# Attention and two feed-forward layers on one Trainium2 core: more weight splits ahead of use, and weight rooms that change hands

## The chip, the cores and the metric

One NeuronCore of a Trainium2 chip runs the whole program. The metric is the device time of one launch in microseconds (us).

## The reference, cut to what matters

```python
def reference(...):
    attn = attention with tanh-capped scores        # 4 batches, 12 heads, 448 tokens, 64 wide
    x = attn as [1792, 768]
    x = (silu(x @ w_gate) * (x @ w_val)) @ w_out     # dense layer, 1536 wide
    do_compute = x @ w_skip > 0                      # tokens that enter the expert layer
    e_idx = argmax(x @ w_route)                      # one of 8 experts for each such token
    for e in range(8):                               # w1[e]: 768 x 1024, w2[e]: 1024 x 768
        h = maximum(x[e_idx == e] @ w1[e], 0)
        y[e_idx == e] = softmax weight * (h @ w2[e])
    out = x, plus y where do_compute
```

## The kernel before

The program runs attention and the dense layer interleaved over four batches, and the expert layer as its last part. Everything is issued in an order written out by hand; each engine runs its own instructions in that order.

The expert layer works in **slots**. A slot holds up to 128 gathered tokens of one expert; a **paired slot** holds 64 tokens of each of two experts. This input uses six slots in this order: 0 to 3 with one expert each, then two paired slots. Slots 0 and 1 are written out word by word in the list `LATE`, mixed with the routing of the last batch (`choose`, `ranks`, `tiles`, `places`, `gates`, `at`, `entries`, `listed`), which runs on VectorE and whose result, the token lists, is needed by the four gathers for the later slots. Slots 2 and up are issued by `slot`, with `so["auto"]` set.

The weights of one expert are eight **pieces** of 768 KB, [128, 1536] in float32: four for w1 (used by `first`, 9 matmuls of 512 columns in float32r) and four for w2 (used by `second`, 12 matmuls of 384 columns). Between them, hidden rows or the next slot's token rows are turned on TensorE (`turn_h`, `turn_x`) and copied out by ScalarE and VectorE. Number the pieces in the order of use: 0 to 7 belong to slot 0, 8 to 15 to slot 1, 16 to 23 and 24 to 31 to slots 2 and 3, 32 to 63 to the two paired slots.

A piece of slots 0 to 3 goes through four steps. `load_next` issues its load on SyncE into a free raw room (`so["raw"]`, 8 of them: three 1536-column pieces of older tiles and five new ones) and puts it on `held`. `split_next` takes the first of `held`, casts it on ScalarE to a high part `gh` (line 1014), subtracts on VectorE to a low part `gl` (line 401), frees the raw room, and puts the two parts on `ready`. The parts take one of seven pairs of rooms (`so["pair"]`); three of the pairs come from the pool "early". `piece`, called by `first` and `second`, takes the first of `ready`; the pair is free again after the matmuls (`used`). A piece of a paired slot **stays whole**: it passes from `held` to `ready` with no cast and no subtraction, is used in float32 straight from its raw room, two pieces (one of each expert) at a time, and frees the raw room only after its matmuls. `first` and `second` then issue half as many columns of weights at a time, two experts side by side.

The lists fill in two ways. In `LATE` the word `split` calls `split_next`. In `slot`, each call of `piece` splits at most one piece, and only while `ready` holds fewer than `AHEAD` = 5.

```python
n = 1
while so["auto"] and held and len(ready) < AHEAD and (not held[0][1] or n and so["pair"]):
    n -= held[0][1]
    split_next()
if not ready:
    split_next()
return ready.pop(0)
```

Seven pieces are split before `LATE` begins, and `LATE` holds nine more splits, so that the last use of slot 1 finds `ready` empty afterwards. A piece is loaded as soon as a raw room is free, but pieces 16 and up wait for the experts of the later slots (`experts`).

Of the kernel before, what the change touches and what calls it, by code (L numbers as in the profile page):

```python
# [7 lines left out]
F32 = mybir.dt.float32  # L8
F32R = mybir.dt.float32r
# [25 lines left out]
AHEAD = 5  # L35
# [30 lines left out]
    chain store  # L66
""".split()
LATE = """
    choose first1 count ranks first2 hidden0 lows0 tiles first3 experts second0 hidden1 lows1 split second1 places
    split second2 rows1 gates split second3 finish0 first0 at split first1 entries split first2 listed0 halves0 split  # L70
    first3 listed1 gather gather gather gather second0 halves1 split second1 rows2 split second2 split second3 finish1
""".split()


# [1 line left out]
def tile_attn_moe_moe(  # L76
# [26 lines left out]
    PIECE = 1536  # L103
# [31 lines left out]
    count = const.tile([T, E], F32, name="count")  # L135
    fit = const.tile([T, 6, E], F32, name="fit")
    early = const.tile([T, FETCHED], F32, name="early")
# [23 lines left out]
    def scratch(room):  # L161
        used = [0]

        def take(*shape):
            n = 1
            for d in shape:
                n *= d
            a = room[:, used[0]:used[0] + n]
            used[0] += n
            assert used[0] <= room.shape[1]  # L170
            if len(shape) == 1:
                return a
            names = " ".join("abc"[:len(shape)])
            return a.rearrange(f"p ({names}) -> p {names}", **dict(zip("abc", shape)))

        return take
# [41 lines left out]
    def gates(b):  # L218
        gt, sh = gate[:, NC * b:NC * b + NC], rt["sh"]
        nc.scalar.activation(out=sh, in_=sh, func=ACTF.Exp)  # L220
        yield V.tensor_reduce(gt, sh, axis=AX.X, op=ALU.add)
        yield V.tensor_scalar(gt, gt, EPS, None, op0=ALU.add)
        yield V.reciprocal(gt, gt)
# [148 lines left out]
    def slot_pieces(e_reg):  # L372
        a = [
            (w1[bass.ds(e_reg, 1), 128 * kk:128 * (kk + 3), 512 * half:512 * half + 512], 3)
            for half in range(F2 // 512) for kk in range(0, KD, 3)
        ]
        return a + [(w2[bass.ds(e_reg, 1), 128 * f:128 * (f + 2)], 2) for f in range(0, KF2, 2)]

    def load_piece(raw, piece):
        src, n = piece  # L380
        nc.sync.dma_start(
            out=raw.rearrange("p (k f) -> p k f", k=n), in_=src.rearrange("o (k p) f -> p (o k) f", p=128)
        )
# [3 lines left out]
    def expert(src):  # L387
        return nc.values_load(src, engines=SP, min_val=0, max_val=E - 1)

    def pieces_of(s):  # L390

        if s < FETCHED:
            return [(p, True) for p in slot_pieces(expert(early_i[0:1, s:s + 1]))]
        if s < MAXWHOLE:
            return [(p, True) for p in slot_pieces(expert(es_i[0:1, s:s + 1]))]
        o = MAXWHOLE + 2 * (s - MAXWHOLE)
        both = zip(*(slot_pieces(expert(es_i[0:1, o + i:o + i + 1])) for i in range(2)))
        return [(p, False) for ps in both for p in ps]

    def split_low(engine, low, full, high):  # L400
        engine.tensor_tensor(low, full, high.bitcast(F32), op=ALU.subtract)  # L401
# [25 lines left out]
    def whole(exact):  # L427
        with ExitStack() as ph:

            def pools(side):  # L430
                stack = ph.enter_context(ExitStack())

                def pool(name, bufs, **kw):
                    kw.setdefault("reuse_waits", "tile")
                    return stack.enter_context(tc.tile_pool(name=name, bufs=bufs, side=side, **kw))

                return stack, pool
# [466 lines left out]
            so = {"raw": [], "pair": [], "xg": [], "auto": False}  # L904

            def open_early():
                qks[0][0].close()
                right.close()
                _, pool = pools("right")
                p = pool("early", 1)  # L910
                psum = pool("ps_e", 1, space=PSUM)
                so["raw"] += [x[:, 0:PIECE] for x in pair_room + [head_room]]
                so["pair"] += [[p.tile([128, PIECE], F32R, name=f"{n}{i}") for n in ("gh", "gl")] for i in range(3)]
                so["odd"] = p.tile([128, PIECE], F32R, name="gl3")
                so["xg"] += [p.tile([128, DM], F32, name=f"xg{i}") for i in range(FETCHED)]
                so["x"] = [p.tile([128, KD, 128], F32R, name=n) for n in ("xgh", "xgl")]
                so["h"] = [[p.tile([128, KF2 // 2, 128], F32R, name=f"{n}{i}") for n in ("rh", "rl")] for i in range(2)]
                so["room"] = p.tile([128, 1024], F32, name="big_room")[0:T]
                so["row"] = p.tile([128, S], F32, name="row2")
                so["ph"] = [psum.tile([128, 512], F32, name=f"ph{i}") for i in range(2)]  # L920
                so["tp"] = [psum.tile([128, 512], F32, name=f"tp{i}") for i in range(2)]
                for xg in so["xg"]:
                    nc.gpsimd.memset(xg, 0.0)
# [62 lines left out]
            def turn_h(half, later=None, n=1):  # L986
                src = so["hid"][:, 512 * half:512 * half + 512]
                if n == 1:
                    turned(*so["h"][half], src, later)
                else:  # L990
                    turned(so["h32"][:, KF2 // 2 * half:KF2 // 2 * (half + 1)], None, src)


            coming, todo, held, ready = [], [], [], []

            def load_next():
                while so["raw"] and not todo:
                    if not coming:
                        return False
                    todo.extend(pieces_of(coming.pop(0)))  # L1000
                if not so["raw"]:
                    return False
                piece_, parted = todo.pop(0)
                held.append((so["raw"].pop(0), parted))
                load_piece(held[-1][0], piece_)
                return True

            def split_next():
                raw, parted = held.pop(0)
                if not parted:  # L1010
                    ready.append((raw,))
                    return
                wh, wl = parts = so["pair"].pop(0)
                nc.scalar.copy(wh, raw)
                split_low(nc.vector, wl, raw, wh)
                so["raw"].append(raw)
                ready.append(parts)
# [9 lines left out]
            def piece():  # L1027
                while load_next():
                    pass

                n = 1
                while so["auto"] and held and len(ready) < AHEAD and (not held[0][1] or n and so["pair"]):
                    n -= held[0][1]
                    split_next()
                if not ready:
                    split_next()
                return ready.pop(0)
# [75 lines left out]
            at = {load_part: 8}  # L1113
# [149 lines left out]
            for word in OPENING:  # L1263
                name = word.rstrip("0123456789")
                x = int(word[len(name):])
# [36 lines left out]
            b, last, take = B - 1, so["last"], scratch(so["late"][0:T])  # L1302

            def all_of(*chains):
                return lambda: [any(False for _ in chain()) for chain in chains]
# [13 lines left out]
            def list_(b0):  # L1319
                for b in range(b0, b0 + 2):  # L1320
                    listed(pl, rhs_[b % 2], rt["rv"][:, NC * b:NC * b + NC], b == 0, b == B - 1)
                    if b < 2:
                        put(b + 2, rhs_[b])
                if b0:
                    to = lists[:, :, FETCHED:]
                    V.tensor_tensor(to, to, pl.rearrange("p (a s) -> p a s", a=2), op=ALU.add)
                    V.tensor_copy(idx[:, FETCHED:], to[:, 0])

            def experts_known():
                yield from experts(take)  # L1330
                coming.extend(order[FETCHED:])
                while load_next():
                    pass

            order = list(range(NWHOLE)) + [MAXWHOLE + i for i in range(NPAIRS)]
            gathered = iter(order[FETCHED:])

# [6 lines left out]
            while load_next():  # L1344
# [4 lines left out]
                "places": all_of(lambda: places(rank, take)), "at": all_of(lambda: last_at(take, room)),  # L1349
                "entries": all_of(entered), "experts": all_of(experts_known),  # L1350
                "listed0": lambda: list_(0), "listed1": lambda: list_(2),
                "gates": all_of(lambda: gates(b)), "split": split_next,
                "hidden0": lambda: turn_h(0, 0), "hidden1": lambda: turn_h(1, 1),
                "lows0": lambda: split_low(V, *lows.pop(0)), "lows1": lambda: split_low(V, *lows.pop(1)),
                "gather": next_gathered, "finish0": lambda: finish(0), "finish1": lambda: finish(1),
# [28 lines left out]
    with tc.manual_schedule():  # L1384
# [57 lines left out]
        with tc.If(big > 0) as cmp:  # L1442
            whole(True)
        with cmp.Else():
            whole(False)
# [31 lines left out]
```

## Time and profile before

| what | value |
|---|---|
| median of 3 runs | 983.2 us (978.3 to 983.58) |
| the profiled execution, its own time | 982.64 us |
| its span, first to last instruction | 980.9 us |
| TensorE busy | 898.1 us (92%) |
| VectorE, ScalarE, GpSimd busy | 580.1, 465.1, 99.1 us |
| mean granted TensorE clock | 0.96 of full speed |
| DMA | 161.55 MB, mean 165 GB/s |

The span lies 1.74 us below the execution's own time. Times in the rows are counted from the start of the span. The granted clock is 1.00 at 2.4 GHz and 0.50 at 1.2 GHz; a stretch with a value between them had some of both. A busy TensorE is not TensorE at its peak, and matmul rows overlap, so steps are read from start to start.

### The profile page before, as it was taken

What the parts mean: (1) busy time and instruction counts of PE and PEld (TensorE: products, weight loads), DVE (VectorE), ACT (ScalarE), POOL (GpSimd) and SP (SyncE); (2) the same over time, 40 slices, a digit from 0 to 9 for tenths busy, and PEclk for the clock granted to TensorE, in tenths of its full rate; (3) what the DMA queues carried; (4) which work ended last, traced back from release to release, by engine and by line L of the source; (5) the groups of instructions that cost most, each with busy time, mean ns of one, the idle gap of its engine ahead of it and who ended that gap; (6) DMA issues with size and microseconds to landing.
All of it is one profiled execution on the core that took longest, in us unless ns stands there. A gap on an engine that the chain in (4) does not pass through costs nothing. (4 is left out here: it accounts for less than half of the span.)

```text
span 980.9 us, 12535 instructions
## 1 busy us (share of the span) xinstructions
PE 898.1 (92%) x4664; PEld 676.4 (69%) x4664; DVE 580.1 (59%) x906; ACT 465.1 (47%) x553; POOL 99.1 (10%) x66
## 2 busy tenths in 40 slices
PE   6899999999999999999999999999999775665984
PEld 2236787776788888778888888999987663544521
DVE  2768899998377666557666743565664943332000
ACT  5887667656464556446555532333342341313100
POOL 1000000000022221212221220000101020000000
PEclk9999999999999999999999999999999988667998
DMA  6996888898764344257343235453376654332894
GB/s 134 195 262 177 221 240 233 227 256 214 185 154 110 84 125 125 57 115 178 94 110 106 65 84 130 134 198 125 90 223 194 211 174 164 108 131 96 310 391 159
DMA packets 226020, 161.55 MB, mean 165 GB/s; under 512 B 158860, under 2 KB 186508, under 8 KB 225936
## 3 DMA queue, kind: packets, MB, share of 16 engines
q1 hardware_dynamic: 224048, 157.12, 57.1%
q0 software_dynamic: 960, 3.16, 0.9%
q8 instruction: 43, 0.70, 0.3%
q14 instruction: 41, 0.34, 0.1%
q10 hardware_dynamic: 928, 0.23, 0.1%
HBM read 140.01 MB, written 22.02 MB: 165 GB/s over the span
## 5 line engine op out<-in xcount | busy, mean ns | idle before, releaser
L748 PE MATMUL mo<-xhl,wh 128*128 128x448 f32 x576 | 215.1, 373 | 0.0
L750 PE MATMUL mo<-xhl,wl 128*128 128x448 f32 x576 | 210.4, 365 | 0.0
L749 PE MATMUL mo<-xhl,wh 128*128 128x448 f32 x576 | 210.3, 365 | 0.0
L401 DVE TENSOR_TENSOR wl<-raw,wh 128x768 fp32r<-128x768 f32 x108 | 117.1, 1084 | 69.8 <-ACT wh L735 69.0
L735 ACT CAST wh<-raw 128x768 fp32r<-128x768 f32 x108 | 89.9, 833 | 76.5 <-PE mo L749 49.5
L748 PEld LDWEIGHTS mo<-xhl,wh 128*128 128x128 f32 x576 | 108.1, 188 | 22.2 <-issue 11.0
L750 PEld LDWEIGHTS mo<-xhl,wl 128*128 128x128 f32 x576 | 108.2, 188 | 8.9 <-DVE wl L401 0.2
L749 PEld LDWEIGHTS mo<-xhl,wh 128*128 128x128 f32 x576 | 108.3, 188 | 7.9
L748 PE MATMUL mo<-hh,wh 128*128 128x448 f32 x288 | 108.2, 376 | 1.1 <-ACT x L795 1.1
L750 PE MATMUL mo<-hh,wl 128*128 128x448 f32 x288 | 105.3, 366 | 0.0
L749 PE MATMUL mo<-hl,wh 128*128 128x448 f32 x288 | 105.3, 366 | 0.0
L787 ACT ACTIVATE s<-mo 128x448 f32<-128x448 f32 x48 | 26.1, 544 | 110.6 <-PE mo L750 107.7
L535 ACT ACTIVATE arena<-ps,inv_sb 112x896 f32<-112x896 f32 x72 | 68.8, 1008 | 4.9 <-PE ps L525 4.9
L542 ACT ACTIVATE arena<-arena,cap_sb 112x1792 f32<-112x1792 f32 x36 | 64.6, 1793 | 1.1
L748 PEld LDWEIGHTS mo<-hh,wh 128*128 128x128 f32 x288 | 54.1, 188 | 11.8 <-issue 4.9
L570 POOL TENSOR_TENSOR sums<-arena 112x896 f32<-112x896 f32 x11 | 23.2, 2111 | 385.7 <-ACT arena L542 385.7
L750 PEld LDWEIGHTS mo<-hh,wl 128*128 128x128 f32 x288 | 54.1, 188 | 4.6
L749 PEld LDWEIGHTS mo<-hl,wh 128*128 128x128 f32 x288 | 54.1, 188 | 4.1
L581 PE MATMUL bank<-arena,arena 112*64 112x448 f32 x264 | 54.9, 548 | 1.3 <-ACT w L706 0.8
L790 DVE SCALAR_TENSOR_TENSOR s<-s,mo 128x448 f32<-128x448 f32 x48 | 29.6, 616 | 32.4 <-PE mo L750 31.5
L706 ACT ACTIVATE w<-raw 128x768 f32<-128x768 f32 x36 | 32.9, 914 | 31.3 <-DVE wl L401 13.6
L1086 DVE SCALAR_TENSOR_TENSOR o<-py,lists,xg 128x768 f32<-128x768 f32 x6 | 6.1, 1017 | 69.3 <-PE py L1050 69.3
(283 smaller groups left out, 1368.6 us busy)
## 6 DMA issues: line engine op xcount, KB each, us to landing
raw<-ws SPq DMA_DIRECT2D x54, 768.0 KB, 4.7
raw<-in_moe_w_dram SPq DMA_DIRECT2D x35, 768.0 KB, 6.4
pair_room<-in_moe_w_dram SPq DMA_DIRECT2D x20, 768.0 KB, 6.0
ws<-w SPq DMA_DIRECT2D x36, 384.0 KB, 5.8
raw<-in_moe_w_gate_dram SPq DMA_DIRECT2D x12, 768.0 KB, 5.9
raw<-in_moe_w_val_dram SPq DMA_DIRECT2D x12, 768.0 KB, 5.5
raw<-in_moe_w_out_dram SPq DMA_DIRECT2D x12, 768.0 KB, 5.1
head_room<-in_moe_w_dram SPq DMA_DIRECT2D x9, 768.0 KB, 5.9
```

Of the source, the lines that this page charges most:

```text
L401: engine.tensor_tensor(low, full, high.bitcast(F32), op=ALU.subtract)
L535: nc.scalar.activation(out=t[:, j], in_=ps[:, :, 0:S], func=ACTF.Tanh, scale=inv_sb[0:T])
L542: nc.scalar.activation(out=ts[part], in_=ts[part], func=ACTF.Exp, scale=cap_sb[0:T])
L570: nc.gpsimd.tensor_tensor(sm, ts[0][:, 0], ts[0][:, 1], op=ALU.add)
L581: nc.tensor.matmul(pv[64 * i:64 * i + 64], lhsT=hd["vn"][:, i, c], rhs=hd["t"][c // 2][:, c % 2, i], start=c == 0, stop=c == NC - 1,)
L706: nc.scalar.activation(out=w32, in_=raws[u][:, :, 1].bitcast(F32), func=ACTF.Abs)
L735: nc.scalar.copy(wh, w32s[w])
L748: nc.tensor.matmul(ps, lhsT=wh, rhs=mh, start=start, stop=False)
L749: nc.tensor.matmul(ps, lhsT=wh, rhs=ml, start=False, stop=False)
L750: nc.tensor.matmul(ps, lhsT=wl, rhs=mh, start=False, stop=stop)
L787: nc.scalar.activation(out=s, in_=cur[op], func=ACTF.Tanh, scale=0.5)
L790: nc.vector.scalar_tensor_tensor(s, in0=s, scalar=0.5, in1=cur.pop(op), op0=ALU.mult, op1=ALU.mult)
```

## The change

`LATE` holds 18 splits in place of 9, and `places` and `gates` stand later in it. The word `split` now does nothing when no piece is held or no pair is free. In `piece` up to two pieces are split for each one that is used, and the limit of five counts only pieces in parts. `load_next`, when no raw room is free and the next piece stays whole and no piece that is to be split is still held, takes a free pair of the three "early" ones out of the pairs for good and turns its two rooms into raw rooms.

```diff
--- before.py
+++ after.py
@@ -66,9 +66,10 @@
     chain store
 """.split()
 LATE = """
-    choose first1 count ranks first2 hidden0 lows0 tiles first3 experts second0 hidden1 lows1 split second1 places
-    split second2 rows1 gates split second3 finish0 first0 at split first1 entries split first2 listed0 halves0 split
-    first3 listed1 gather gather gather gather second0 halves1 split second1 rows2 split second2 split second3 finish1
+    choose first1 count ranks first2 hidden0 lows0 tiles first3 experts second0 hidden1 lows1 split second1 split
+    split second2 rows1 split second3 finish0 split first0 places split gates split first1 at split first2 halves0
+    entries split split first3 split listed0 second0 halves1 split listed1 gather gather gather gather split second1
+    split rows2 split second2 split split second3 finish1 split
 """.split()
 
 
@@ -910,7 +911,11 @@
                 p = pool("early", 1)
                 psum = pool("ps_e", 1, space=PSUM)
                 so["raw"] += [x[:, 0:PIECE] for x in pair_room + [head_room]]
-                so["pair"] += [[p.tile([128, PIECE], F32R, name=f"{n}{i}") for n in ("gh", "gl")] for i in range(3)]
+                so["pair"] += [
+                    [p.tile([128, PIECE], F32R, tag=f"{n}{i}", name=f"{n}{i}") for n in ("gh", "gl")] for i in range(3)
+                ]
+
+                so["lent"], so["early"] = list(so["pair"]), p
                 so["odd"] = p.tile([128, PIECE], F32R, name="gl3")
                 so["xg"] += [p.tile([128, DM], F32, name=f"xg{i}") for i in range(FETCHED)]
                 so["x"] = [p.tile([128, KD, 128], F32R, name=n) for n in ("xgh", "xgl")]
@@ -994,10 +999,20 @@
             coming, todo, held, ready = [], [], [], []
 
             def load_next():
-                while so["raw"] and not todo:
+                if so["raw"] and not todo:
                     if not coming:
                         return False
                     todo.extend(pieces_of(coming.pop(0)))
+
+                if not so["raw"] and todo and not todo[0][1] and not any(x[1] for x in held):
+                    for i, parts in enumerate(so["lent"]):
+                        if any(parts is x for x in so["pair"]):
+                            so["pair"] = [x for x in so["pair"] if x is not parts]
+                            so["lent"][i] = None
+                            so["raw"] += [
+                                so["early"].tile([128, PIECE], F32, tag=f"{n}{i}", name=f"{n}{i}_whole") for n in ("gh", "gl")
+                            ]
+                            break
                 if not so["raw"]:
                     return False
                 piece_, parted = todo.pop(0)
@@ -1028,8 +1043,10 @@
                 while load_next():
                     pass
 
-                n = 1
-                while so["auto"] and held and len(ready) < AHEAD and (not held[0][1] or n and so["pair"]):
+                n = 2
+                while so["auto"] and held and (
+                    not held[0][1] or n and so["pair"] and sum(len(x) > 1 for x in ready) < AHEAD
+                ):
                     n -= held[0][1]
                     split_next()
                 if not ready:
@@ -1332,6 +1349,12 @@
                 while load_next():
                     pass
 
+            def split_if():
+                while load_next():
+                    pass
+                if held and so["pair"]:
+                    split_next()
+
             order = list(range(NWHOLE)) + [MAXWHOLE + i for i in range(NPAIRS)]
             gathered = iter(order[FETCHED:])
 
@@ -1349,7 +1372,7 @@
                 "places": all_of(lambda: places(rank, take)), "at": all_of(lambda: last_at(take, room)),
                 "entries": all_of(entered), "experts": all_of(experts_known),
                 "listed0": lambda: list_(0), "listed1": lambda: list_(2),
-                "gates": all_of(lambda: gates(b)), "split": split_next,
+                "gates": all_of(lambda: gates(b)), "split": split_if,
                 "hidden0": lambda: turn_h(0, 0), "hidden1": lambda: turn_h(1, 1),
                 "lows0": lambda: split_low(V, *lows.pop(0)), "lows1": lambda: split_low(V, *lows.pop(1)),
                 "gather": next_gathered, "finish0": lambda: finish(0), "finish1": lambda: finish(1),
```

## Rows read from the trace of the kernel before

**Rows 1.** The page's strips, 40 slices of 24.5 us: granted clock, DMA share

```profile
PEclk9999999999999999999999999999999988667998
DMA  6996888898764344257343235453376654332894
```

**Rows 2.** By stage: length, busy us of the five engines, clock, DMA share, GB/s

```profile
770.00:812.50 42.50, 28.42 (x133) 24.01 (x131) 27.35 (x46) 14.53 (x15) 7.25 (x6) 0.88 0.56 184
812.50:862.50 50.00, 30.79 (x98) 24.70 (x98) 17.20 (x14) 14.18 (x14) 2.26 (x2) 0.73 0.41 134
862.50:912.50 50.00, 33.06 (x98) 26.05 (x98) 13.94 (x10) 11.53 (x12) 1.30 (x1) 0.66 0.38 129
912.50:936.80 24.30, 24.19 (x129) 9.49 (x128) 1.04 (x2) 3.23 (x6) 0.98 (x1) 1.00 0.89 334
936.80:970.20 33.40, 27.60 (x119) 9.63 (x118) 0.99 (x1) 2.37 (x4) 0.98 (x1) 1.00 0.89 337
970.20:980.90 10.70, 0.01 (x1) 0.00 (x0) 1.02 (x1) 0.00 (x0) 0.98 (x1) 0.72 0.10 31
```

**Rows 3.** All engines in order of time, one piece of the third expert slot

```profile
833.33 1.46 ACT L1014 CAST gh<-raw 128x1536 fp32r<-128x1536 f32 x1
834.83 1.76 DVE L401 TENSOR_TENSOR gl<-raw,gh 128x1536 fp32r<-128x1536 f32 x1 [5.92 <-ACT gh L1014]
...
834.85 0.69 PE L1050 MATMUL py<-gh,rh 128*128 128x384 f32 x1 [2.11 <-ACT gh L1014]
...
836.64 0.69 PE L1050 MATMUL py<-gl,rh 128*128 128x384 f32 x1 [1.11 <-DVE gl L401]
...
837.13 0.52 PE L1050 MATMUL py<-gh,rl 128*128 128x384 f32 x1
...
840.33 1.05 PE L966 MATMUL tp<-ident,hid 128*128 128x128 f32 x4
```

**Rows 4.** Who waited for whom, 810 to 912.5 us; us in all, times, longest

```profile
PE py L1050 <- ACT gh L1014: 12.2, 6, 2.1
```

**Rows 5.** TensorE in order of time: two turns and one piece, full clock

```profile
761.42 0.60 PE L966 MATMUL tp<-ident,hid 128*128 128x128 f32 x4
761.78 0.42 PE L1050 MATMUL py<-gh,rh 128*128 128x384 f32 x1
...
767.33 0.82 PE L966 MATMUL tp<-ident,xg 128*128 128x128 f32 x6
767.90 0.42 PE L1050 MATMUL py<-gh,rh 128*128 128x384 f32 x1
...
770.07 0.39 PE L1050 MATMUL ph<-gh,xgh 128*128 128x512 f32 x1
```

**Rows 6.** Busy time by engine, a stretch unbroken after a wait

```profile
853.40:858.70 5.30, 5.30 (x17) 5.30 (x18) 1.62 (x1) 2.28 (x2) 0.00 (x0) 0.50 0.75 226
```

**Rows 7.** Busy time by engine, routing stretch

```profile
764.70:790.30 25.60, 19.52 (x103) 16.74 (x104) 23.30 (x45) 9.30 (x11) 1.03 (x1) 0.93 0.52 170
```

**Rows 8.** VectorE in order of time: the lists' end, two subtractions in a row

```profile
790.10 0.18 DVE L1327 CAST idx<-lists 128x22 uint32<-128x22 f32 x1
...
811.14 1.75 DVE L401 TENSOR_TENSOR gl<-head_room,gh 128x1536 fp32r<-128x1536 f32 x1
812.81 1.75 DVE L401 TENSOR_TENSOR more<-pair_room,more 128x1536 fp32r<-128x1536 f32 x1
```

**Rows 9.** The gathered rows' tile: its gathers, ns, first and last start; landing

```profile
L952 POOL DMA_INDIRECT xg<-out_dram,idx x4: 1008/1026/2164, 791.1 to 795.1; - x4
...
DMA to landing us min/median/max: 4.0/5.8/7.5
```

**Rows 10.** The page's DMA issues: one load of a weight piece

```profile
raw<-in_moe_w_dram SPq DMA_DIRECT2D x35, 768.0 KB, 6.4
```

**Rows 11.** SyncE in order of time where loads begin to run unbroken

```profile
908.36 0.37 SPq L381 DMA_DIRECT2D pair_room<-in_moe_w_dram  x1
915.32 0.38 SPq L381 DMA_DIRECT2D head_room<-in_moe_w_dram  x1
```

**Rows 12.** Busy time by engine and GB/s, the paired slots

```profile
915.00:965.00 50.00, 45.20 (x219) 16.97 (x216) 1.02 (x1) 5.59 (x10) 0.98 (x1) 1.00 1.01 380
```

## Prediction

> **What bounds the kernel now.** I read the strips of the page first, then busy time by stage, then one piece of weights in order of time, then who waits for whom, and last the loads. In the strips the granted clock stands at 9 for 32 slices and then falls to 8, 8, 6, 6, 7 before it comes back, while the DMA strip stands at 2 to 6 and reaches 8 and 9 only in slices 38 and 39 [rows 1]: the kernel is held up in the expert layer, and the stages tell three things of it. From 770 to 912.5 us (slots 1 to 3) TensorE has 92.3 us of rows in 142.5 us and no other engine is near full; from 812.5 on, VectorE has 31.1 us of 100 and DMA a share near 0.4, at a granted clock of 0.66 to 0.73 [rows 2]. From 912.5 to 970.2 us (the paired slots) the clock is 1.00, and DMA runs without pause: its share over 915 to 965 us is 1.01 at 380 GB/s [rows 12]. From there to the end of the span, 10.7 us of finishing follow [rows 2].
>
> One piece shows the first stretch. The cast starts at 833.33 and takes 1.46, the subtraction starts at 834.83 and takes 1.76; TensorE waits 2.11 us for the one, issues a single matmul, and waits 1.11 for the other [rows 3]. Nothing was split ahead: cast, subtraction and matmuls stand in a chain. The waits on casts in `second` alone are 12.2 us in six times [rows 4]. The other loss is the clock: after the waits 11 matmuls of this piece take 3.69 us (836.64 to 840.33), and after another wait 5.3 unbroken us still run at 0.50 [rows 3, 6]; a whole piece at the full clock takes 2.17 (767.90 to 770.07) [rows 5]. So the wait that ends last is lack of lead in slots 1 to 3, and the loads in the paired slots.
>
> **What the change does to the lead.** I counted the lists through by hand. After `second0` of slot 0, `ready` holds 2 in both versions. Before, nine splits meet nine uses and slot 1 ends with `ready` at 0; then `piece` splits one and uses one, so the lead stays 0 although `AHEAD` is 5. After, 16 of the 18 splits find a piece and a pair (two find no pair and do nothing), and slot 1 ends with 7 ready, pieces 16 to 22. In slots 2 and 3 `piece` then keeps five ready before each use, four behind it. The second split per piece hardly acts, since the lead comes from `LATE`; it would rebuild one that was lost. No cast or subtraction is added in all; they move forward.
>
> **Slot 1, which pays for it.** VectorE works in order, and six more subtractions (of pieces 13 to 18) now stand ahead of the token lists. A subtraction adds 1.67 us when it follows another (811.14 to 812.81) [rows 8]: 6 x 1.67 = 10.0. In the stretch concerned VectorE has 23.3 of 25.6 us filled, so at most 2.3 of it hides [rows 7]. The lists end at 790.28 now [rows 8], and after at 798.0 to 800.3; I take 799.3. Queued behind them are the gathers, and behind these the turn of slot 2's tokens, which stands on TensorE ahead of the last two pieces of slot 1. The gather starts 0.8 after the lists and lands 4.0 to 7.5 us later, 5.8 in the median [rows 8, 9]: 805.9. Then the turn and two pieces: TensorE has waited, so I price the turn at 1.1 and one piece at the half clock, 4.0 (3.69 for 11 matmuls [rows 3]), and the next at 2.2. Slot 1 ends at 799.3 + 0.8 + 5.8 + 1.1 + 4.0 + 2.2 = 813.2. Moving `places` and `gates` costs nothing of its own: the same instructions, in the same queue, ahead of `at` and `entries`, which use them; without that cover it would be the few us that VectorE has between the lists and the gathers.
>
> **Slots 2 and 3.** With four pieces split ahead, a split has about 8 us until its use, against 1.46 + 1.76 = 3.2 [rows 3]. Eight pieces at 2.17, two turns of hidden rows at 0.36 (761.42 to 761.78) and one of tokens at 0.57 (767.33 to 767.90) [rows 5] are 18.7 us a slot, if the clock stays full, which unbroken work gives in the paired slots [rows 2]. Casts are 1.46 and subtractions 1.76 per 2.17, so neither engine becomes the bound. Two slots: 37.4, and the paired slots begin at 850.6. Now they begin at 912.5.
>
> **The paired slots.** TensorE alone needs 24.3 for the first, in which it hardly waited (24.19 of 24.3) [rows 2], and some 23.5 for the second, without the next turn: 47.8, to 898.4. The loads: now the unbroken run begins with the issue at 915.32, of piece 40 (908.36 is piece 39, and eight rooms then hold 32 to 39) [rows 11]; 24 pieces later TensorE is done, at 970.2, 54.9 us on. A piece of 768 KB [rows 10] at 380 GB/s [rows 12] is 2.07. After the change piece 31 is split while piece 27 is used, five pieces and two turns (5 x 2.17 + 0.36 + 0.57 = 11.8) ahead of the paired slots, plus 3.2 for the split: 842.0. That frees the room for piece 39, and the lent rooms follow from there, six of them by the time the last parts are used. So the run is 25 pieces from 842.0: 842.0 + 54.9 + 2.07 = 899.0. Loads and TensorE end together; I take 899.0. A lent room's load waits on SyncE for TensorE's last use of the pair, but a pair is lent only once it is free, so that wait is nothing to a few tenths.
>
> The Trainium skill, "DMA: Bandwidth & Descriptors", section Specifications, gives an HBM limit of about 358 GB/s per core, which speaks against so early an end; by it the 25 pieces would take about 55 us in place of 52, an estimate from that page, and the end would be some 3 us later. The trace does not agree: 380 GB/s over 50 us [rows 12].
>
> **The sum.** Slots 1 to 3: 770 to 850.6 in place of 912.5, 61.9 less. Paired slots: 850.6 to 899.0, 48.4 in place of 57.7, 9.3 less. Span 980.9 - 71.2 = 909.7, and with the 1.74 us around it 911.4, from an execution of 982.64, which is 0.56 below the median. I predict 911 us.
>
> **Rivals.**
> - *The lead thins at the turns.* ScalarE also copies turned rows and takes its casts in order behind them; if each of the three turns of a slot cost a full chain of 3.2, that is 2 x 3 x 3.2 = 19: 930 us. For it: today these copies and casts are neighbours on ScalarE. Against: the piece between a turn and its use covers 2.17.
> - *The rooms come too late.* If lending gives nothing, piece 40 waits for the first paired step (24.3 / 8 = 3.0): 850.6 + 3.0 + 54.9 = 908.5, so 9.5 later, 921 us. Against: the pairs are free by then.
> - *The clock stays at half* through slots 2 and 3: each eight pieces at 4.0 and doubled turns, 34.6, so 2 x 15.9 = 32 more: 943 us. Against: 1.00 wherever TensorE is not made to wait [rows 2].
> - *Slower: splits outrun the loads.* A split of a piece just issued holds ScalarE until the landing, 6.4 [rows 10]; a piece then costs 6.4 + 3.2 + 2.2 = 11.8 in place of 100 / 16 = 6.3 [rows 2], 16 x 5.5 = 88 above now: about 1,070 us. It decides from the point where the wait for landings passes some 4.5 us at every piece, which uses up the 71 us. Against: a split frees the room of the piece eight further on, and eight subtractions last 13.4, more than 6.4.
> - *The change does nothing:* the new splits find no piece or no pair, the lead stays 0: 983 us. Against: the count above.
>
> **How the numbers follow.** Forecast 0.64, turns 0.15, rooms 0.12, clock 0.05, slower 0.02, nothing 0.02. The forecast's own bounds: with lists at 798.0, gathers in 4.0 and no half clock, slot 1 ends some 6 us earlier, 905; a few us more if waits I counted vanish. Upward, the gather at 7.5 and lists at 800.3 add 3. To hold 8 in 10 the range takes in the rooms and the turns: 900 to 932. A measurement here tells about 0.5% from no change, some 5 us; only the last two rivals are not faster by that: faster 0.96, same 0.02, slower 0.02.
>
> **What would show it.** In the profile after: lists near 799; TensorE idle for some 5 us or more ahead of slot 2's turn; no waits on `gh` or `gl` in slots 2 and 3, each under 20 us, at a granted clock of 1.00; loads unbroken from about 842; paired slots in 48 us. It is wrong if waits on casts remain after slot 1, if the clock stays near 0.7, or if the lists come far later than 800.

## The result and the profile after

The changed kernel takes 914.32 us in the median of four runs (913.83 to 916.38), the kernel before 980.76 us in the runs beside it: a ratio of 0.9326, with a 95% interval of 0.9289 to 0.9363. The forecast of 911 us was 3 us low; the gain was 66 us where 71 was forecast. The profiled execution took 914.07 us, its span is 912.2 us.

The strips of the page of the kernel after: granted clock and DMA share, 40 slices of 22.8 us.

```profile
PEclk9999999999999999999999999999999999689998
DMA  6897789878958335433844322453532768768993
```

The clock now falls in two slices, to 6 and 8, where it fell in five to 6 to 8 before [rows 1] (the last slice, 8 in both, holds the end of the matmuls). Which stage that is, busy time by stage says (slot 1; slot 2; slot 3; the two paired slots; the end; columns as in [rows 2]; each slot is counted from its first weight matmul):

```profile
770.00:813.60 43.60, 26.50 (x126) 24.47 (x125) 31.17 (x50) 16.73 (x17) 7.84 (x5) 0.73 0.72 255
813.60:831.70 18.10, 18.10 (x99) 16.51 (x98) 13.52 (x12) 12.28 (x13) 2.29 (x1) 1.00 0.69 215
831.70:850.00 18.30, 18.30 (x101) 16.43 (x99) 10.48 (x8) 8.07 (x10) 2.26 (x1) 1.00 0.98 353
850.00:873.10 23.10, 23.10 (x127) 9.31 (x128) 1.02 (x1) 3.22 (x6) 0.99 (x1) 1.00 1.04 393
873.10:901.30 28.20, 24.98 (x122) 9.28 (x118) 1.07 (x2) 2.37 (x4) 0.98 (x1) 1.00 0.85 324
901.30:912.20 10.90, 0.00 (x0) 0.00 (x0) 0.97 (x1) 0.00 (x0) 0.98 (x1) 0.71 0.11 30
```

Slots 2 and 3 take 18.1 and 18.3 us, each filled by TensorE from end to end at a clock of 1.00. In the kernel before they took 102.5 us, from 810.01 to 912.50, with TensorE rows in 64 of the 100 us of [rows 2]. The first weight matmul of slot 2, before and after:

```profile
810.01 0.40 PE L1050 MATMUL ph<-gh,xgh 128*128 128x512 f32 x1
...
813.58 0.39 PE L1067 MATMUL ph<-gh,xgh 128*128 128x512 f32 x1
```

So slots 2 and 3 give 66 of the 68.7 us by which the span is shorter, the paired slots give 6.5, and slot 1 takes 3.6 back. Slot 1 has become the stage with the low clock (0.73), and the paired slots, 51.3 us, still hold waits in the second one: 24.98 of 28.20.

Two waits make up all the idle time of TensorE in slot 1, 17.1 of 43.6 us. TensorE in order of time, the rows with an idle time of over 1 us:

```profile
787.45 3.64 PE L266 MATMUL last<-big_room,late_room 112*128 112x44 f32 x16 [10.04 <-DVE late_room L254]
...
807.26 1.54 PE L971 MATMUL tp<-ident,xg 128*128 128x128 f32 x6 [7.06 <-DMA xg<-out_dram,idx]
```

It waits 10.04 us for VectorE, which works through routing and subtractions in turn, and 7.06 us for the gathered rows. On VectorE the lists end at 800.03, where they ended at 790.28 [rows 8]:

```profile
799.62 0.19 DVE L1343 TENSOR_TENSOR lists<-lists,last 128x44 f32<-128x44 f32 x1
799.85 0.18 DVE L1344 CAST idx<-lists 128x22 uint32<-128x22 f32 x1
```

### The profile page after: what moved, and what is told of

Read it like the earlier page. It is cut to its first block, busy times and chain, and to the rows that moved or that the text cites. A ratio compares the mean times of both kernels' runs of the same rounds, so it can differ in the third digit from the quotient of the medians.

```text
span 912.2 us, 12534 instructions
## 1 busy us (share of the span) xinstructions
PE 866.4 (95%) x4664; PEld 659.4 (72%) x4664; DVE 578.4 (63%) x906; ACT 465.3 (51%) x553; POOL 100.6 (11%) x66
## 5 line engine op out<-in xcount | busy, mean ns | idle before, releaser
L582 PE MATMUL bank<-arena,arena 112*64 112x448 f32 x264 | 54.9, 548 | 1.6 <-ACT arena L543 0.8
L526 PE MATMUL ps<-qkt 64*112 64x448 f32 x208 | 45.9, 560 | 0.0
```

The source lines that it names most:

```text
L526: nc.tensor.matmul(ps[:, i, 0:S], lhsT=ks[rows_, 1, T * c:T * c + T], rhs=qs[rows_, 0], start=y == 0, stop=y == len(terms_) - 1,)
L582: nc.tensor.matmul(pv[64 * i:64 * i + 64], lhsT=hd["vn"][:, i, c], rhs=hd["t"][c // 2][:, c % 2, i], start=c == 0, stop=c == NC - 1,)
```

## Experiments

Eleven kernels ran. The before beside them had medians of 980 to 982 us, so each is given with its ratio.

**The doubled list alone.** The new `LATE` and the new word `split`; in `piece` and in the rooms everything as before.

```diff
-                n = 2
-                while so["auto"] and held and (
-                    not held[0][1] or n and so["pair"] and sum(len(x) > 1 for x in ready) < AHEAD
-                ):
+                n = 1
+                while so["auto"] and held and len(ready) < AHEAD and (not held[0][1] or n and so["pair"]):
...
-                so["lent"], so["early"] = list(so["pair"]), p
+                so["lent"], so["early"] = [], p
```

> The doubled list alone, with the old rule for a piece and no rooms lent. If the lead comes from the list (my theory), slot 1 ends with seven pieces ready, slots 2 and 3 take some 35 us as in the kernel after, and only the paired slots lose the six early rooms: the unbroken loads then begin one paired step (3 us) after the paired slots do, and 54.9 us later TensorE is done: 850 + 3 + 54.9 = 908 in place of 901, so about 921 us. If it takes the second split per piece to keep a lead, slots 2 and 3 fall back to some 100 us and the time is 970 or more. If the rooms are what pays, it is near 980.

Measured: 921.84 us, 0.9398 (0.9368 to 0.9427). The list gives 60 of the 66 us by itself. Its slots 2 and 3 take 36.4 us (812.82 to 849.25), as in the kernel after.

**No room lent.** The second half of the diff above alone, in the kernel after.

> The kernel after with no room lent. My sum prices the lent rooms at the difference of 850 + 3 + 54.9 = 908 and 901: about 921 us, 7 more than after, with slots 2 and 3 unchanged and TensorE waiting on landings in the paired slots. If the loads are hidden anyway it is 914; if the rooms also fed slots 2 and 3, more than 930.

Measured: 923.29 us, 0.9411 (0.9382 to 0.944). Busy time in slots 2 and 3 together and in each paired slot:

```profile
812.40:848.80 36.40, 36.40 (x197) 32.95 (x196) 24.02 (x19) 20.33 (x22) 4.55 (x2) 1.00 0.80 258
848.80:873.20 24.40, 23.53 (x127) 9.99 (x128) 1.02 (x1) 3.23 (x6) 0.98 (x1) 1.00 0.87 320
873.20:906.80 33.60, 27.49 (x123) 9.77 (x120) 1.05 (x2) 2.37 (x4) 0.98 (x1) 1.00 0.90 339
```

Slots 2 and 3 are as in the kernel after; the paired slots take 58.0 us in place of 51.3, so the lent rooms are worth 6.7 us in the profiles (9 in the medians), and only there. The kernel with the list alone has the old rule for a piece besides and takes 1.5 us less, no more than the scatter here (919.52 to 924.85). The new limit, which counts only pieces in parts, was not tried by itself with the lent rooms.

**One split for a piece used.**

```diff
-                n = 2
+                n = 1
```

> The kernel after with one split for a piece used in place of two. If the lead comes from the list, the second split never decides and the time is that of the kernel after within 2 us, 914. If the second split is what holds the lead, waits on casts come back in slots 2 and 3 and it is 930 or more.

Measured: 915.65 us, 0.9331 (0.93 to 0.9362): no difference from the kernel after. With the doubled list the second split decides nothing.

**The old list with the new rule and the lent rooms.** `LATE` is that of the kernel before, all else that of the kernel after.

> The old list of nine splits, with the new rule for a piece (up to two splits for one used) and the lent rooms. If only the list can give the lead, slots 2 and 3 wait on casts as before and the time is near 970. If the rule refills the lead by itself, slot 1 ends at about 810 as before (its lists are ready at 790, not 800), and since a subtraction follows another in 1.67 us and a piece takes 2.17 on TensorE, the lead is back after some four pieces at a cost of about 4 us: paired slots from about 850 and about 914 us, no worse than the kernel after. I hold the second for likelier, 0.7; it would mean that the doubled list is not needed.

Measured: 917.82 us, 0.9356 (0.9327 to 0.9385). The rule refills the lead. Slot 2, slot 3, and what TensorE waited for from 790 us on:

```profile
809.60:834.60 25.00, 20.56 (x100) 17.58 (x99) 21.97 (x17) 14.90 (x15) 2.29 (x1) 0.93 0.84 308
834.60:852.80 18.20, 18.20 (x99) 16.34 (x97) 10.39 (x8) 7.97 (x10) 2.26 (x1) 1.00 1.04 384
```

```profile
793.40 0.68 PE L1066 MATMUL py<-gh,rh 128*128 128x384 f32 x1 [2.05 <-ACT gh L1028]
795.20 0.69 PE L1066 MATMUL py<-gl,rh 128*128 128x384 f32 x1 [1.12 <-DVE gl L401]
802.30 0.44 PE L1066 MATMUL py<-gh,rh 128*128 128x384 f32 x1 [1.94 <-ACT gh L1028]
804.10 0.69 PE L1066 MATMUL py<-gl,rh 128*128 128x384 f32 x1 [1.35 <-DVE gl L401]
812.52 0.50 PE L1066 MATMUL ph<-gl,xgh 128*128 128x512 f32 x1 [2.54 <-DVE gl L401]
824.40 0.45 PE L1066 MATMUL py<-gh,rl 128*128 128x384 f32 x1 [1.18 <-DVE rl L401]
830.00 0.55 PE L970 MATMUL tp<-ident,xg 128*128 128x128 f32 x3 [0.72 <-DVE rl L401]
```

The waits on casts end with slot 1; in slot 2 one wait on a subtraction of weights stands at its start, and two on turned rows behind subtractions. Slot 2 pays 6.9 us more than in the kernel after, where I expected 4, and slot 1 ends 4 us earlier (809.58, not 813.58). Of the 6.9 us, 4.4 are these three waits (2.54, 1.18 and 0.72); the nine matmuls from 813.78 to 817.43, behind the first wait, take 3.65 us where nine take 2.04 at the full clock (815.66 to 817.70 in the kernel after), 1.6 more. So there are two ways to the same lead, and the kernel after has both.

**The lent rooms alone.** The kernel before with the lending of the kernel after.

> The kernel before with the lent rooms alone: old list, old rule for a piece. By my sum the lead is what pays and the rooms only shorten the paired slots: these begin near 912 as before, take some 50 us in place of 58, and the time is about 973 us. If the rooms pay for more than that, 960 or less; if they need the lead to be of use, 980.

Measured: 977.57 us, 0.9948 (0.9925 to 0.997), about 5 us less where 9 were expected. Slots 2 and 3 keep a clock near 0.7 and their waits. The loads from piece 39 on and the paired slots:

```profile
911.90 0.37 SPq L381 DMA_DIRECT2D pair_room<-in_moe_w_dram  x1
912.52 0.37 SPq L381 DMA_DIRECT2D gh_whole<-in_moe_w_dram  x1
...
916.00:939.10 23.10, 23.10 (x127) 9.35 (x128) 1.02 (x1) 3.22 (x6) 0.98 (x1) 1.00 1.03 394
939.10:971.00 31.90, 26.99 (x122) 9.80 (x119) 1.02 (x1) 2.37 (x4) 0.98 (x1) 1.00 0.86 324
```

The paired slots take 55.0 us, not some 50. Without a lead the last split comes just before its use, and only then are the rooms lent: piece 39 is issued 4.1 us ahead of the paired slots, in the kernel after 7.7 us (842.32, and 850.00). From that load to the last matmul it is 59.1 us here (970.96) and 58.9 there (901.21). So the rooms give less here because they are lent later: the lead brings the loads forward too.

**Matmuls left out of the paired slots.** Three of the eight row blocks of w2 are left out in each; all loads stay.

```diff
-                for f in range(2):
+                for f in range(2 if n == 1 or i == 3 else 1):
```

> The kernel after with three of the eight row blocks of w2 left out of the matmuls in each paired slot, all loads kept. That takes 3 x 1.28 = 3.8 us of TensorE from each paired slot, 7.7 in all. If loads set the end of the paired slots, as the waits on landings in the last one say, the end moves by 0 to 1 us, 914; if TensorE sets it, 907.

Measured: 914.33 us, 0.9306 (0.9264 to 0.9348). TensorE has 7.7 us less to do and the time does not move. The paired slots by busy time:

```profile
853.40:872.80 19.40, 19.40 (x104) 7.71 (x106) 1.04 (x2) 3.23 (x6) 0.98 (x1) 1.00 1.04 394
872.80:904.60 31.80, 24.01 (x96) 7.57 (x92) 1.00 (x1) 2.37 (x4) 0.98 (x1) 1.00 0.87 330
```

The first is 3.7 us shorter, the second 3.6 us longer, 51.2 us in all. From the load of piece 39, issued at 845.64, to the last matmul at 904.59 it is 58.95 us, as in the kernel after: the loads set the end.

**Short loads in the paired slots.** Whole pieces load only a third (w1) or a half (w2) of their columns, except the first into each lent room; all matmuls stay, on what the rooms held.

```diff
+        if short:
+            nc.sync.dma_start(
+                out=raw.rearrange("p (k f) -> p k f", k=n)[:, 0:1],
+                in_=src.rearrange("o (k p) f -> p (o k) f", p=128)[:, 0:1],
+            )
+            return
...
-                load_piece(held[-1][0], piece_)
+                load_piece(held[-1][0], piece_, not parted and any(held[-1][0] is x for x in full))
+                full.append(held[-1][0])
```

> The kernel after with the loads of whole pieces cut to a third (w1) or a half (w2), except the first load into each lent room; all matmuls kept, on what the rooms held. If the loads set the end of the paired slots by a little and TensorE stands right behind them, the waits on landings go, the paired slots take 23.2 + 24 = 47 us in place of 51.1, and the time is 910 to 911. If it is far more than loads (TensorE could be much faster), it is below 905; if loads do not matter, 914.

Measured: 907.26 us, 0.925 (0.9216 to 0.9284), 7 us less than the kernel after where 3 to 4 were expected. The paired slots:

```profile
850.60:873.80 23.20, 23.20 (x128) 9.36 (x130) 1.02 (x1) 3.22 (x6) 0.98 (x1) 1.00 0.85 308
873.80:896.00 22.20, 22.09 (x120) 8.42 (x116) 1.05 (x2) 2.36 (x4) 0.98 (x1) 1.00 0.24 82
```

TensorE, busy in 45.29 of 45.40 us, needs 45.4 us for both. The loads cost the kernel after 5.9 us there.

**The lists before the additional splits.** To take back what slot 1 pays, the order of the kernel before is kept up to the gathers, and the splits that are added stand behind them.

```diff
+    choose first1 count ranks first2 hidden0 lows0 tiles first3 experts second0 hidden1 lows1 split second1 places
+    split second2 rows1 gates split second3 finish0 first0 at split first1 entries split first2 listed0 halves0 split
+    first3 listed1 gather gather gather gather split split second0 halves1 split split second1 split second2 rows2
+    split second3 split finish1 split
```

> The kernel after with another list: the order of the kernel before up to the gathers, and the additional splits behind them (six more than before, one word moved). If the 10 us of subtractions ahead of the token lists are what slot 1 pays, the lists are ready at 790 again in place of 800, the gathered rows land near 797, and slot 1 ends near 801 in place of 815, with two or three pieces split ahead that the rule for a piece brings to five. Slots 2 and 3 keep some 36 us, the paired slots begin near 837, the loads run unbroken from near 828, and the time is about 900 us (898 to 905). If a lead of seven at the end of slot 1 is needed, slot 2 takes 26 us as in the kernel with the old list and the new rule, and it is 908 or more. If the loads alone set the end, it stays at 914.

Measured: 905.56 us, 0.921 (0.9182 to 0.9238): 9 us less than the kernel after, 5 short of what I expected. The list has 14 splits, five more than before, where the expectation says six. Busy time from the routing on (slot 1 is over and slot 2 begins in the second row):

```profile
765.00:790.00 25.00, 19.73 (x87) 16.83 (x86) 20.70 (x41) 7.72 (x10) 1.03 (x1) 0.80 0.52 173
790.00:807.00 17.00, 14.75 (x88) 13.77 (x88) 14.85 (x14) 13.82 (x13) 6.76 (x4) 1.00 0.84 293
807.00:824.00 17.00, 16.14 (x89) 14.62 (x89) 16.36 (x14) 14.02 (x15) 2.29 (x1) 1.00 1.04 388
824.00:841.00 17.00, 17.00 (x95) 15.36 (x96) 9.13 (x8) 6.72 (x9) 2.26 (x1) 1.00 1.04 391
841.00:864.30 23.30, 23.30 (x128) 9.36 (x130) 1.05 (x2) 3.22 (x6) 0.98 (x1) 1.00 1.04 393
864.30:893.70 29.40, 26.15 (x120) 9.50 (x116) 0.98 (x2) 2.36 (x4) 0.98 (x1) 1.00 0.81 309
```

The lists are ready at 792 (790 before, 800 in the kernel after), slot 1 ends at 803.4 and the paired slots begin at 840.9. But the loads now run at 388 to 393 GB/s from slot 2 on, and the last slot pays with 29.4 us. What is left lies in the first row: 173 GB/s, with rooms full of pieces that wait for VectorE.

**A longer lead on top of it.** `AHEAD = 7` in place of 5, else the same.

> The kernel lists_first with a limit of seven pieces in parts in place of five, which frees up to two raw rooms two pieces (some 4 us) earlier. If the end of the paired slots is set by the loads, up to 4 us less than lists_first, about 897; if TensorE sets it there, no change.

Measured: 905.34 us, 0.9217 (0.9182 to 0.9251), no change, by a trade: slots 2 and 3 take longer, with waits of 2.9 and 1.1 us at turned rows (the first paired slot starts at 843.7, not 840.9), and the last one is shorter (25.0 us).

**Rooms lent from the start.** On top of the lists' order, one or two of the three early pairs become raw rooms as soon as the experts of the later slots are known; the lending in `load_next` then passes over them. With two:

```diff
                 yield from experts(take)
+                for i in range(2):
+                    so["pair"] = [x for x in so["pair"] if x is not so["lent"][i]]
+                    so["lent"][i] = None
+                    so["raw"] += [
+                        so["early"].tile([128, PIECE], F32, tag=f"{n}{i}", name=f"{n}{i}_soon") for n in ("gh", "gl")
+                    ]
```

> The kernel lists_first with one of the three early pairs turned into two raw rooms as soon as the experts of the later slots are known, in place of near the end of slot 3. In lists_first the loads run at 390 GB/s from about 805 us to the end and set it, while at 765 to 790 they ran at 173 GB/s for want of a free room. If so, two loads moved into that stretch take 2 x 2.0 = 4 us off the end, until TensorE sets it: it needs some 47.9 us from the start of the paired slots (841.0), so 889 in place of 893.7. About 901.5 us against 905.6. If six pairs are too few for the lead, waits on casts come back in slot 2 and it is 907 or more.

> The same with two of the three early pairs, four rooms: 8 us of loads earlier, of which TensorE's own 889 lets 4.8 count. About 901 us, no better than with one pair; five pairs left for parts may cost some us of waits in slots 2 and 3.

Measured: 901.26 us with one pair, 0.9189 (0.9158 to 0.922), as expected; 897.66 us with two, 0.9145 (0.9117 to 0.9173), 3 us better than expected. With two, the routing stretch and the two halves of the end:

```profile
765.00:790.00 25.00, 19.71 (x105) 16.96 (x104) 22.41 (x44) 10.07 (x12) 1.03 (x1) 0.86 0.75 272
...
837.00:862.00 25.00, 25.00 (x139) 11.13 (x139) 1.02 (x1) 3.23 (x6) 0.98 (x1) 1.00 0.95 347
862.00:887.00 25.00, 23.33 (x124) 8.76 (x120) 2.04 (x2) 2.37 (x4) 0.98 (x1) 1.00 0.76 291
```

The routing stretch now loads at 272 GB/s in place of 173, and five pairs are enough for the lead. The last matmuls end at 885.8. The paired slots begin at 839.1, where I had put 841.0, and take 46.7 us, where I had put 47.9; TensorE by itself needs 45.4. This version beats both kernels, by 17 us the one after.

## Why the prediction was right

- **The lead.** Shown. The list alone gives 921.84 us, and with it slots 2 and 3 have no wait on a cast. That the second split hardly acts is shown by 915.65 us without it; that it would rebuild a lost lead, by 917.82 us with the old list.
- **Slot 1.** The lists were put at 799.3 and ended at 800.03; the turn was put at 805.9 and began at 807.26, since the gathers took 6.3 to 6.7 us to land, not the 5.8 of before [rows 9]; the end was put at 813.2 and came at 813.58. That this is 0.4 us off is in part luck: the turn began 1.4 us late, and the turn and two pieces behind it took 6.3 us where I had 7.3, since the clock came back within the first piece (matmuls 0.32 us apart, and 0.17 from 810.45 on). That the six subtractions ahead of the lists are the cause is shown by the kernel that puts the lists first: ready at 792, slot 1 over at 803.4, and the paired slots begin 9 us earlier.
- **Slots 2 and 3.** 37.4 us forecast, 36.4 measured; I had priced every piece at 2.17, the piece that has a turn ahead of it, and others take 2.08 (829.65 to 831.73). The clock came back to 1.00 as forecast. The paired slots were put at 850.6 and began at 850.0.
- **The paired slots: the step that was mis-sized.** 48.4 us forecast, 51.2 measured to the end of the last matmuls, 901.2 in place of 899.0. The load of piece 39 was put at 842.0 and was issued at 842.32, with the lent rooms right behind it:

```profile
842.32 0.37 SPq L382 DMA_DIRECT2D pair_room<-in_moe_w_dram  x1
842.93 0.37 SPq L382 DMA_DIRECT2D gh_whole<-in_moe_w_dram  x1
843.51 0.37 SPq L382 DMA_DIRECT2D gl_whole<-in_moe_w_dram  x1
```

  But I took the run of 54.9 us from the kernel before, where piece 39 had landed when piece 40 was issued [rows 11]. Here five loads had been issued in the 11 us before and were in part still on their way. What the load queue moved from piece 40 to the end in the kernel before (915.32 on), and from piece 39 to the end in the kernel after (842.3 on; packets, MB, share):

```profile
q1 hardware_dynamic: 7552, 18.88, 90.8%
...
q1 hardware_dynamic: 8625, 20.97, 93.5%
```

  The first is 24 pieces of 0.786 MB and nothing more; the second is 25 pieces, 19.66 MB, and 1.3 MB of earlier ones. At 394 GB/s these are 3.3 us that the forecast lacked; in the kernel before, loads also began slowly (156 GB/s over 915.3 to 918.0), which the run of 54.9 us holds and the kernel after does not pay, some 1.6 us. Both are estimates from these rows; the run took 58.9 us from piece 39 where I had 57.0. And TensorE was not level with the loads: short loads show 45.4 us for it, where I had 47.8. So the loads bind by 6 us; I had them end together. Over the span the errors are +0.4 (slot 1), -1.0 (slots 2 and 3), +2.8 (paired slots) and +0.3 us (the end): 912.2 where the sum had 909.7.
- **The rivals.** Waits at the turns did not come: slots 2 and 3 are full. The clock did not stay at half. Rooms too late is what the kernels without lending show, 921.84 and 923.29, as its price of 921 says; without lending the paired slots take 57.9 us from their first matmul to their last (848.81 to 906.73), and the price was 3.0 + 54.9. Splits did not outrun the loads, and no split waited on a landing in a way that reached TensorE.
- **The limit of the loads.** Over 842 to 892 us DMA moved 394 GB/s:

```profile
842.00:892.00 50.00, 49.01 (x264) 23.87 (x265) 3.02 (x4) 7.04 (x13) 1.98 (x2) 1.00 1.04 394
```

  The Trainium skill's figure of about 358 GB/s per core ("DMA: Bandwidth & Descriptors", Specifications) is there a stack's rate divided by its two cores, and it is not what bounds a core that runs alone here, so the prediction need not have set it against its own 380 GB/s; the measurement decides.

What stays open: whether the new limit, which counts only pieces in parts, does anything beside the lent rooms; how much the lent rooms are worth exactly (9 us in the medians, 6.7 in the profiles, of which the one without lending is the fastest of its four executions); and the last 0.9 of the 6.9 us that slot 2 pays with the old list.

## What to carry to other kernels

A rule that makes one and uses one never builds a lead, whatever its limit says: count the lists through by hand, and look for the place that makes more than is used. Work moved forward on an in-order engine delays what stands behind it there; put it behind the results that others wait for. Once the stalls were gone here, the loads bound: look for the stretch in which DMA is half idle for want of a room, and let rooms change hands there.

## What was not expected of the hardware

The gathers for the later slots landed in 6.3 to 6.7 us under a DMA share of 0.72 in slot 1, where they took 4.0 to 7.5 before [rows 9]; with the lists put first, 6.3 to 7.8. A core alone held 388 to 393 GB/s over three stages in a row, 57 us (807 to 864.3 with the lists put first), with no sign of a fall.
